# A fused attention and two-layer kernel: all steps put in a new order, found in a replay whose TensorE stops every 127 products

## The chip, the cores and the metric

The kernel runs on one core of a Trainium2 chip. The metric is device microseconds (us) of one execution; lower is better. TensorE (PE) multiplies matrices and loads its stationary operand as a separate step (PEld); VectorE (DVE), ScalarE (ACT) and GpSimd (POOL) do the element-wise work; SyncE (SP) issues the DMAs.

## What is computed

Windowed attention, then a layer with a softmax-weighted activation and a layer norm, then a layer with a sigmoid-gated activation, all in float32:

```
# attention: 4 batches, 8 heads, 576 positions, 64 wide
scores = scale * q @ k.T, masked: heads 0-3 the last 32 positions,
                          heads 4-7 every 4th of the last 128
x = softmax(scores) @ v                      # 2304 tokens x 512

# layer 1: 512 -> 1024 -> 512
h = x @ w_in
solu = h * softmax(h)
ln = (solu - mean) / sqrt(var + 1e-6) * g_ln
x = ln @ w_out

# layer 2: 512 -> 2048 -> 512
h = x @ w_in2
g = h * (1 / (1 + exp(-1.702 * h)))
out = g @ w_out2
```

## The kernel before

**Numbers.** A float32 product is made of three products in a shorter format: high by high, high by low, low by high. So each operand is split: a copy to the short format is its high part, and the difference is its low part. The splits are `split_hi` and `split_lo` for layer 1's weights (L506 to L530), `moe_xh` and `moe_xl` for x, `moe_lnh` and `moe_lnl` for ln (L625, L628), `unit_hi` and `unit_lo` (L696, L700) for the weights of layer 2, and `o_hi` and `o_lo` (L809, L812) for g. The lows of `w_out` carry the factor g_ln and are the tile `wo_l` (L530), the highs `wo_h` (L518 on POOL, L520 on ACT).

**Attention** goes by blocks of one batch and a pair of heads. `att_s` (L276) makes the scores s: up to 64 small products on corners of the array, with the mask added by one product of an identity (L288, L300). The mask, the maximum (`mx`, L324, L327), the exponential and the norm (L362 to L369) follow; `att_t` (L371) transposes the probabilities into a bank called ptp; `att_p` copies them to SBUF (L388, the tiles `diag` and `pt`); and `att_x` (L391) multiplies them by v (xt, L406, L421, L424).

**Layer 1** goes by tiles of 128 tokens. `moe_h` (L549) makes h in two halves of 12 products into one of two large PSUM banks, which is free again when `moe_solu` (L574) has written e (L577). Behind it come the layer norm, four transposes `lt` (L618) and, for each group of tiles, y in 24 products (L638).

**Layer 2** runs in three passes, each over a pair of blocks of 384 tokens, for 8 quads of weight blocks, with seven products in place of eight for each 2 by 2 block. `h_prod` (L762) makes hx and hz; sums and gates follow on DVE, POOL and ACT (L767 to L805), and `o_prod` (L844) multiplies the split g (the tiles `gs`) by the weights `wo` and `w`. The weights of layer 2 are summed and split once (L682 to L700), written to DRAM (`unit_store`, L704, into `wdq` and `wdo`) and read from there for every use (`quad_load` L709; `o_load` L819, the tiles `wo`; `o_load2` L829).

**What sets the order.** Each step is a `Work` of the class `Plan`, with an engine, sometimes other engines that could do it, a cost in us, the steps it needs, and the buffers that it takes and gives back. The list `ORDER` names all 2394 steps in turn; `PICKS` says which steps use a second or third engine. `replay` walks the engines' queues in that order with the costs, and the program is written out in the order of the replayed starts. So both tables, and through the replay also the costs, set what stands before what on each engine. The replay sets one more thing: before a PE step that is marked warm (scores, transposes, xt, h) it counts how long PE would wait, and `stir` (L270) puts that many dummy products of an identity, up to 12, into the bank which the step is about to fill. In the replay PE also waits where a block of instructions must be fetched: every BLOCK products, the first after BLOCK0, no earlier than FETCH us behind the start of the product 32 places ahead.

Of the kernel before, what the change touches and what calls it, by code (L numbers as in the profile page):

```python
# [48 lines left out]
HOP, DMA_RATE, DMA_IN, DMA_OUT, ISSUE, LANES, FETCH, BLOCK, BLOCK0 = 0.035, 360e3, 2.3, 1.0, 0.43, 8, 2.55, 128, 94  # L49
COLD, EARLY, LATE_RATE = 7.5, 60.0, 320e3  # L50
# [14 lines left out]
class Plan:  # L65
# [15 lines left out]
    def replay(self):  # L81
# [15 lines left out]
        port, land, lanes, ld, mms, left = 0.0, 0.0, [0.0] * LANES, 0, [], len(order)  # L97
        while left:
# [32 lines left out]
            if e == "PE":  # L131
# [7 lines left out]
                end, cost = t, w.cost * (2 if t < COLD else 1)  # L139
                for _ in range(w.mm):  # L140
                    if (len(mms) - BLOCK0) % BLOCK == 0 and len(mms) >= 32:
                        end = max(end, mms[-32] + FETCH)
                    mms.append(end)
                    end += cost / w.mm
# [34 lines left out]
def attention_moe_kernel(ctx, tc, qk, qk_last, v, v_last, masks, w_in, w_out, g_ln, w2_in, w2_out, out):  # L179
# [806 lines left out]
    for c in range(8):  # L986
        r, w = at["w", c], done["w", c]
        if (w_out if c >= 4 else w_in).dtype == I64:
# [3 lines left out]
                          ("POOL", 1.115 if c < 4 else 1.35, lambda c=c: split_hi(c, nc.gpsimd))])  # L992
# [11 lines left out]
    for i in range(NTILE):  # L1004
# [24 lines left out]
        w = add(r, "ACT", 1.4, lambda i=i: moe_var(i), [w, z])  # L1029
        w = add(r, "POOL", 0.62, lambda i=i: moe_rs(i), [w])  # L1030
        w = add(r, "ACT", 1.4, lambda i=i: moe_ln(i), [w], port=True,
# [37 lines left out]
    for k in (1, 2, 3):  # L1069
        w_after = [end[n] for n in range(4)] if k < 3 else [closed]  # L1070
        raw, hl = (("raw", k), ("hl", k)) if k < 3 else ("raw", "hl")
        for n, u in enumerate(PARK[k]):
# [8 lines left out]
            for i in range(3):  # L1081
                w = add(r, "POOL", 0.41 if i else 0.69, lambda u=u, i=i: unit_sum(u, i, nc.gpsimd), [w], port=True,
                        also=[("DVE", 0.29 if i else 0.42, lambda u=u, i=i: unit_sum(u, i, nc.vector))])
            lo_ = None
            for part in range(2):
                fin = part == 1

                def split(copy, k=k, u=u, part=part):
# [4 lines left out]
                        also=[("DVE", 0.42 if fin else 0.35, lambda s=split: s(nc.vector.tensor_copy)),  # L1093
# [251 lines left out]
def plan_sequence():  # L1345
# [74 lines left out]
ORDER = [4, 1, 78, 79, 80, 81, 19, 88, 89, 90, 5, 8, 57, 58, 59, 60, 3, 263, 68, 91, 92, 93, 94, 262, 82, 61, 62, 0, 47, 48,  # L1420
# [239 lines left out]
```

## Time and profile before

| | us |
|---|---|
| three runs, median (lowest to highest) | 645.27 (644.74 to 646.63) |
| the profiled execution's own time | 646.25 |
| its span in the trace, first to last instruction | 644.5 |
| PE busy (5065 products) | 626.5 |
| DVE busy | 459.9 |
| ACT busy | 324.2 |
| POOL busy | 257.1 |

The span is that of one execution, recorded by the hardware. An engine's busy time counts its computing instructions alone. The chain of waits goes back from the last instruction to what released it, and so on to the start; its shares say what the time was spent on. A row of a wait tells the engine and line that waited, what came last, the total, how many times, and the longest. In a stretch the columns are its length, the busy time of the engine (with its instructions), the clock that TensorE was granted as a share of full speed (2.4 GHz; one half is 1.2), the share of DMA time and the traffic in GB/s. A few per cent of the products can be missing from the records.

### The profile page before, as it was taken

To read this page: it belongs to the slowest core of one execution; us is meant where nothing else is said; L and a number is where in the kernel's file an instruction comes from. 1 tells how busy PE (TensorE), PEld (TensorE's weight loads), DVE (VectorE), ACT (ScalarE), POOL (GpSimd) and SP (SyncE) were. 2 spreads that over 40 slices of the span, in tenths; PEclk is the share of its full clock that TensorE was granted. 3 is DMA by queue.
4 is the path that set the end of the run, shared out by engine and by line. 5 is a ranking of instruction groups with operands and counts; after the bars stand their busy time and mean duration, and the time that the engine had idled before them with its cause. 6 is when DMAs were issued, how large, how long until landed. Compare 5 with 4: busy or idle time off the path is not lost.

```text
span 644.5 us, 13119 instructions
## 1 busy us (share of the span) xinstructions
PE 626.5 (97%) x5065; PEld 588.8 (91%) x5065; DVE 459.9 (71%) x817; ACT 324.2 (50%) x706; POOL 257.1 (40%) x282
## 2 busy tenths in 40 slices
PE   6889999999999999999999999999999999999997
PEld 3678789889899899999999899999999999999997
DVE  3878998876787976663779969434678963448795
ACT  4689977776475564714547443322454213243331
POOL 2557546454444434655353244204123240026220
PEclk9889999999999999999999999999999999999999
DMA  8899326763667448635988998677898966868584
GB/s 319 319 376 406 116 101 221 255 212 131 216 241 255 178 149 271 235 124 174 321 291 298 343 344 296 236 253 261 275 331 261 330 206 216 290 255 296 186 262 163
DMA packets 65006, 161.36 MB, mean 250 GB/s; under 512 B 6960, under 2 KB 28592, under 8 KB 64944
## 3 DMA queue, kind: packets, MB, share of 16 engines
q1 hardware_dynamic: 64944, 160.53, 71.4%
q8 instruction: 40, 0.66, 0.4%
q14 instruction: 22, 0.18, 0.1%
HBM read 126.42 MB, written 34.08 MB: 249 GB/s over the span
## 4 chain that ended last, share of the span: by engine, by line
PE 82%; DVE 7%; DMA 4%; ACT 3%; issue 2%; POOL 1%; SPq 0%; POOLq 0%; DVEq 0%; ACTq 0%
PE y L638 15%; PE hz L762 15%; PE oz L844 14%; PE hx L762 11%; PE h L557 11%; PE ox L844 9%; PE lt L618 2%; DMA wo<-wdo 2%; DMA wdq<-hl_('q', 7, 1)_0_4305 1%; PE s L292 1%; PE xt L406 1%; DVE e L577 1%; PE ptp L377 1%; DVE gs L812 1%; DMA qk<-in_qk_dram 1%
## 5 line engine op out<-in xcount | busy, mean ns | idle before, releaser
L809 ACT CAST gs<-g 128x384 fp32r<-128x384 f32 x115 | 57.9, 513 | 87.7 <-DVE g L805 37.0
L638 PE MATMUL y<-ln_t,wo_h 128*128 128x384 f32 x384 | 98.4, 337 | 0.0
L762 PE MATMUL hz<-yc,ws 128*128 128x384 f32 x492 | 97.6, 335 | 0.0
L812 DVE TENSOR_TENSOR gs<-g,gs 128x384 fp32r<-128x384 f32 x133 | 80.2, 621 | 21.8 <-ACT gs L809 15.9
L762 PEld LDWEIGHTS hz<-yc,ws 128*128 128x128 f32 x492 | 86.3, 188 | 0.1
L762 PE MATMUL hx<-yc,ws 128*128 128x384 f32 x369 | 74.4, 335 | 0.0
L638 PEld LDWEIGHTS y<-ln_t,wo_h 128*128 128x128 f32 x384 | 69.0, 188 | 0.7
L812 POOL TENSOR_TENSOR gs<-g,gs 128x384 fp32r<-128x384 f32 x35 | 38.8, 1113 | 72.1 <-ACT gs L809 70.4
L762 PEld LDWEIGHTS hx<-yc,ws 128*128 128x128 f32 x369 | 64.8, 188 | 0.2 <-ACT p L767 0.2
L638 PE MATMUL y<-ln_t,wo_l 128*128 128x384 f32 x192 | 64.3, 335 | 0.0
L805 POOL TENSOR_TENSOR g<-g,g 128x384 f32<-128x384 f32 x25 | 28.4, 1142 | 80.2 <-DVE g L805 44.9
L557 PE MATMUL h<-wi_h,xh 128*128 128x512 f32 x144 | 59.0, 410 | 0.9 <-DVE e L577 0.9
L844 PE MATMUL ox<-gs,wo 128*128 128x384 f32 x288 | 55.7, 337 | 1.5 <-DVE gs L812 1.2
L557 PE MATMUL h<-wi_l,xh 128*128 128x512 f32 x144 | 56.6, 393 | 0.0
L557 PE MATMUL h<-wi_h,xl 128*128 128x512 f32 x144 | 56.6, 393 | 0.0
L844 PE MATMUL oz<-gs,wo 128*128 128x384 f32 x288 | 55.2, 335 | 0.1
L844 PE MATMUL oz<-gs,w 128*128 128x384 f32 x288 | 53.4, 336 | 0.0
L844 PEld LDWEIGHTS ox<-gs,wo 128*128 128x128 f32 x288 | 50.2, 188 | 3.0 <-DVE gs L812 2.5
L844 PEld LDWEIGHTS oz<-gs,wo 128*128 128x128 f32 x288 | 50.3, 188 | 0.7 <-DVE gs L812 0.7
L844 PEld LDWEIGHTS oz<-gs,w 128*128 128x128 f32 x288 | 50.1, 188 | 0.7 <-DVE gs L812 0.6
L805 DVE TENSOR_TENSOR g<-g,g 128x384 f32<-128x384 f32 x71 | 43.5, 622 | 5.9 <-ACT g L795 3.4
L795 ACT ACTIVATE g<-g 128x384 f32<-128x384 f32 x72 | 35.0, 520 | 22.6 <-DVE g L771 14.3
(420 smaller groups left out, 1203.2 us busy)
## 6 DMA issues: line engine op xcount, KB each, us to landing
wo<-wdo SPq DMA_DIRECT2D x48, 512.0 KB, 5.5
ws<-wdq SPq DMA_DIRECT2D x41, 512.0 KB, 5.4
w<-wdo SPq DMA_DIRECT2D x72, 256.0 KB, 5.1
ws<-wdq SPq DMA_DIRECT2D x41, 384.0 KB, 4.8
qk<-in_qk_dram SPq DMA_DIRECT2D x14, 528.0 KB, 7.3
v<-in_v_dram SPq DMA_DIRECT2D x14, 512.0 KB, 7.5
out_dram<-ob SPq DMA_DIRECT2D x11, 384.0 KB, 4.7
w_t<-in_w_in_dram SPq DMA_DIRECT2D x8, 512.0 KB, 7.6
```

What stands on the lines that cost most here:

```text
L292: nc.tensor.matmul(ps[QB * j:QB * j + QB, h, m * KW:m * KW + KW], q_[rows, c:c + QB], k_[rows, c:c + KW], start=not masked, stop=not maske ...
L377: nc.tensor.transpose(ps[:, j * P:j * P + P], t[:, 2 * j:2 * j + 2, :].rearrange("p m k -> p (m k)"), ident)
L406: nc.tensor.matmul(o, vW[4 * b + u][:, h, 4 * c + j, :], x, start=True, stop=True, tile_position=(0, 64 * h))
L557: nc.tensor.matmul(hps[i][:, half, :], x[:, kt, :], w[:, kt, fs], start=(kt == 0 and j == 0), stop=(kt == KT - 1 and j == 2))
L618: nc.tensor.transpose(ps[:, j, :], es[i][:, f * P:f * P + P], ident)
L638: nc.tensor.matmul(yps[g, dm][:, 0:TG].rearrange("p (t n) -> p t n", t=GT), w[:, f, ds_], x[:, :, f, :], start=(f == 0 and j == 0), stop=( ...
L762: nc.tensor.matmul(ps[:, 0:TB2], quad_weights(p, q, m, kk, a), yc2[m][:, x, kk, :], start=(m < 4 and kk == 0 and i == 0), stop=(kk == 1 an ...
L795: nc.scalar.activation(g_tile(q, 0, 0) if (half, b) == (0, 0) else src, src, AF.Gelu_apprx_sigmoid)
L805: eng.tensor_tensor(o_block(jj, *o), o_block(jj, *x), o_block(jj, *y_), op)
L809: copy(gsp[jj, m][:, 0], o_block(jj, half, b))
L812: eng.tensor_tensor(gsp[jj, m][:, 1], o_block(jj, half, b), f32(gsp[jj, m][:, 0]), ALU.subtract)
L844: nc.tensor.matmul(ps, w, gsp[jj, m][:, x], start=m < 4 and first and i == 0, stop=last and i == 2, skip_group_check=True)
```

## The change

Constants of the replay and some costs of the planner change, and both tables are new, found in a search that replays with them. No step computes anything else than before. The diff without the rows of the two tables (one line of each stands for it):

```
-HOP, DMA_RATE, DMA_IN, DMA_OUT, ISSUE, LANES, FETCH, BLOCK, BLOCK0 = 0.035, 360e3, 2.3, 1.0, 0.43, 8, 2.55, 128, 94
-COLD, EARLY, LATE_RATE = 7.5, 60.0, 320e3
+HOP, DMA_RATE, DMA_IN, DMA_OUT, ISSUE, LANES, FETCH, BLOCK, BLOCK0 = 0.035, 360e3, 2.3, 1.0, 0.43, 8, 3.2, 127, 95
+COLD, EARLY, LATE_RATE, TURN = 7.5, 60.0, 320e3, 0.095
...
-        port, land, lanes, ld, mms, left = 0.0, 0.0, [0.0] * LANES, 0, [], len(order)
+        port, land, lanes, ld, mms, left, last = 0.0, 0.0, [0.0] * LANES, 0, [], len(order), 0
...
+                kind = 2 if w.mm >= 32 else int(w.mm in (2, 4))
+                if last and not kind or kind == 2 and not last and len(mms) > 12:
+                    end += TURN
+                last = kind
...
-                          ("POOL", 1.115 if c < 4 else 1.35, lambda c=c: split_hi(c, nc.gpsimd))])
+                          ("POOL", 1.115 if c < 4 else 3.25, lambda c=c: split_hi(c, nc.gpsimd))])
...
-        w = add(r, "ACT", 1.4, lambda i=i: moe_var(i), [w, z])
-        w = add(r, "POOL", 0.62, lambda i=i: moe_rs(i), [w])
-        w = add(r, "ACT", 1.4, lambda i=i: moe_ln(i), [w], port=True,
+        w = add(r, "ACT", 1.56, lambda i=i: moe_var(i), [w, z])
+        w = add(r, "POOL", 0.55, lambda i=i: moe_rs(i), [w])
+        w = add(r, "ACT", 1.57, lambda i=i: moe_ln(i), [w], port=True,
...
-                w = add(r, "POOL", 0.41 if i else 0.69, lambda u=u, i=i: unit_sum(u, i, nc.gpsimd), [w], port=True,
+                w = add(r, "POOL", 0.43 if i else 0.86, lambda u=u, i=i: unit_sum(u, i, nc.gpsimd), [w], port=True,
...
-                        also=[("DVE", 0.42 if fin else 0.35, lambda s=split: s(nc.vector.tensor_copy)),
+                        also=[("DVE", 0.42 if fin else 0.545, lambda s=split: s(nc.vector.tensor_copy)),
...
-ORDER = [4, 1, 78, 79, 80, 81, 19, 88, 89, 90, 5, 8, 57, 58, 59, 60, 3, 263, 68, 91, 92, 93, 94, 262, 82, 61, 62, 0, 47, 48,
+ORDER = [4, 1, 78, 13, 79, 80, 14, 81, 82, 19, 88, 89, 90, 8, 57, 58, 59, 0, 47, 91, 92, 93, 5, 68, 60, 61, 62, 3, 262, 263,
...
-PICKS = {53: 1, 65: 1, 67: 1, 74: 1, 75: 1, 96: 1, 105: 1, 124: 1, 137: 1, 156: 1, 158: 1, 169: 1, 181: 1, 191: 1, 200: 1,
+PICKS = {51: 1, 74: 1, 82: 1, 85: 1, 87: 1, 92: 1, 94: 1, 96: 1, 105: 1, 106: 1, 114: 1, 124: 1, 129: 1, 137: 1, 140: 1,
```

Behind its two constants the changed file has four lines more, so its lines carry numbers higher by 4 (L557 is L561). What the new tables do in numbers:

| in the program | before | changed |
|---|---|---|
| products on PE, dummies among them | 5065, 15 | 5070, 20 |
| changes between small and wide products on PE, in the replay's sense | 133 | 127 |
| rows on DVE, ACT, POOL | 793, 570, 277 | 797, 542, 296 |
| pieces of `wo_h` on POOL, ACT | 2, 6 | 0, 8 |
| norm steps of attention (L369, L373 changed) on POOL, DVE | 15, 5 | 9, 11 |
| lows of g (L812) on POOL, DVE | 35, 133 | 41, 127 |

**PE near the 730th product.** The rows of scores (s) with 32 products count twice, so that one group is 64. The 730th product is in the last row of scores of the first list, and falls behind the last transposes (ptp) in the second. Before:

```order
L377 MATMUL ptp_732<-ident,t_612 128x128 x2
L288 LDWEIGHTS ident_b
L288 MATMUL s_736<-mk,ident_b 128x256
L288 LDWEIGHTS ident_b
L288 MATMUL s_736<-mk,ident_b 128x256
L292 MATMUL s_736<-qk_607 32x64 x32
L421 MATMUL xt_0_786<-pt_772,vl_399 64x4x8
```

Changed:

```order
L296 MATMUL s_692<-qk_493 32x64 x32
L381 MATMUL ptp_733<-ident,t_607 128x128 x2
L278 LDWEIGHTS ident_b
L278 MATMUL xt_0_746<-ident_b 128x512
L278 LDWEIGHTS ident_b
L278 MATMUL xt_0_746<-ident_b 128x512
L425 MATMUL xt_0_746<-pt_742,vl_414 64x4x8
L428 MATMUL xt_1_747<-pt_742,vl_414 64x32
```

The score group now stands ahead of the transposes, and the xt behind them has two dummies (L278) in its bank first. At the 349th product it is alike: behind eight transposes came a score, and now come two dummies and an xt.

**DVE between the third and the fourth e of layer 1.** Before:

```order
L577 SCALAR_TENSOR_TENSOR e_1247,mu_1265<-h_1089,e_1247 128x1024
L546 TENSOR_TENSOR xl_1269<-xr,xh_1226 128x512
L530 SCALAR_TENSOR_TENSOR wo_l<-w_t,g_sb,wo_h 128x512 x2
L696 CAST park_hl<-y_early 128x4x128
L530 SCALAR_TENSOR_TENSOR wo_l<-w_t,g_sb,wo_h 128x512 x2
L565 TENSOR_REDUCE nm_1297<-h_1208 128x1
L324 TENSOR_REDUCE mx_1327<-t_1062 128x8
L315 SCALAR_TENSOR_TENSOR t_1337<-s_1310,mk 128x256
L324 TENSOR_REDUCE mx_1357<-t_1337 128x4
L625 CAST ln_t<-lt_0_1301 128x512
L577 SCALAR_TENSOR_TENSOR e_1354,mu_1374<-h_1208,e_1354 128x1024
```

Changed:

```order
L581 SCALAR_TENSOR_TENSOR e_1267,mu_1275<-h_1074,e_1267 128x1024
L534 SCALAR_TENSOR_TENSOR wo_l<-w_t,g_sb,wo_h 128x512 x2
L569 TENSOR_REDUCE nm_1298<-h_1207 128x1
L328 TENSOR_REDUCE mx_1310<-t_1202 128x8
L366 TENSOR_REDUCE sum_eps_110<-t_1067 128x8
L367 TENSOR_REDUCE sx_1338<-sum_eps_110 128x8
L368 RECIPROCAL sx_1338<-sx_1338 128x8
L480 SCALAR_TENSOR_TENSOR y_early<-y_early 128x512
L373 TENSOR_TENSOR t_1067<-t_1067,sx_1338 128x512
L581 SCALAR_TENSOR_TENSOR e_1365,mu_1378<-h_1207,e_1365 128x1024
```

One of two pairs of `wo_l`, a step of x (xl), a copy for layer 2 and a copy of lt have gone from between the two, and a norm of attention and half a weight conversion have come.

**SP ahead of the first o products.** The weight loads (`wo`, two halves for each quad) and the stores of the last split weights (`wdq`, `wdo`). Before:

```order
L673 DMA raw_('o', 5, 1)_4354<-in_w_out_dram 128x1024
L819 DMA wo_0_1_4365<-wdo_124 128x1024
L819 DMA wo_1_1_4367<-wdo_125 128x1024
L819 DMA wo_1_0_4378<-wdo_125 128x1024
L704 DMA wdq_123<-hl_('q', 7, 1)_0_4305 128x768
L819 DMA wo_6_1_4458<-wdo_130 128x1024
L819 DMA wo_6_0_4464<-wdo_130 128x1024
L819 DMA wo_2_1_4489<-wdo_126 128x1024
L819 DMA wo_2_0_4493<-wdo_126 128x1024
L704 DMA wdo_129<-hl_('o', 5, 1)_0_4536 128x768
```

Changed:

```order
L677 DMA raw_('o', 5, 1)_4315<-in_w_out_dram 128x1024
L708 DMA wdq_123<-hl_('q', 7, 1)_0_4280 128x768
L708 DMA wdq_123<-hl_('q', 7, 1)_1_4286 128x1024
L823 DMA wo_0_1_4339<-wdo_124 128x1024
L823 DMA wo_0_0_4381<-wdo_124 128x1024
L823 DMA wo_1_1_4384<-wdo_125 128x1024
L823 DMA wo_1_0_4395<-wdo_125 128x1024
L823 DMA wo_6_1_4454<-wdo_130 128x1024
L823 DMA wo_6_0_4459<-wdo_130 128x1024
L708 DMA wdo_127<-hl_('o', 3, 0)_0_4489 128x768
L823 DMA wo_2_1_4511<-wdo_126 128x1024
L823 DMA wo_2_0_4514<-wdo_126 128x1024
```

The store of quad 7's last weights goes ahead of the `wo` loads, and one store of (o,3,0) ahead of the load of `wo_2`.

## Rows read from the trace of the kernel before

**Rows 1.** Page, part 1: busy us (share of the span), instructions.
```profile
span 644.5 us, 13119 instructions
PE 626.5 (97%) x5065; PEld 588.8 (91%) x5065; DVE 459.9 (71%) x817; ACT 324.2 (50%) x706; POOL 257.1 (40%) x282
```

**Rows 2.** Page, part 4: the chain that ended last, by engine.
```profile
PE 82%; DVE 7%; DMA 4%; ACT 3%; issue 2%; POOL 1%; SPq 0%; POOLq 0%; DVEq 0%; ACTq 0%
```

**Rows 3.** Stretches: length, PE busy (products), clock, DMA share, GB/s.
```profile
0.00:13.92 13.92, 7.87 (x222) 1.00 0.88 305
13.92:19.99 6.07, 3.83 (x127) 1.00 1.02 405
19.99:36.65 16.66, 13.51 (x381) 0.90 0.86 295
36.65:39.74 3.09, 3.08 (x100) 0.56 1.00 407
39.74:160.00 120.26, 119.03 (x1523) 1.00 0.60 220
160.00:340.00 180.00, 179.96 (x1007) 1.00 0.65 224
340.00:380.00 40.00, 38.37 (x212) 1.00 0.92 329
380.00:640.90 260.90, 260.87 (x1501) 1.00 0.77 261
```

**Rows 4.** Waits of PE: us in total, times, longest us.
```profile
PE s L292 <- issue: 3.7, 2, 1.8
...
PE s L288 <- DVE mx L327: 2.1, 1, 2.1
...
PE h L557 <- DVE e L577: 0.9, 1, 0.9
PE xt L406 <- DVE diag L388: 0.9, 1, 0.9
```

**Rows 5.** Page, part 3: the queue that fetches instructions.
```profile
q8 instruction: 40, 0.66, 0.4%
```

**Rows 6.** Timeline of PE, 19 to 41 us: start, length, line, what.
```profile
21.63 1.93 PE L406 MATMUL xt<-diag,v 128*64 128x64 f32 x32
26.08 1.15 PE L406 MATMUL xt<-diag,y_early 128*64 128x64 f32 x32 [0.18 <-ACT diag L388]
```

**Rows 7.** Chain, 100 to 180 us: start, length, what.
```profile
119.80 2.95 PE h L557 x12
129.02 2.77 PE h L557 x12
```

**Rows 8.** Groups of instructions: count, busy us, mean ns, idle before.
```profile
L274 PE MATMUL s<-ident_b 128*128 128x512 bf16 x10 | 4.3, 596 | 2.6 <-POOL ident_b L201 2.6
L518 POOL TENSOR_SCALAR wo_h<-w_t,g_sb 128x512 fp32r<-128x512 f32 x2 | 3.7, 1877 | 0.0
```

**Rows 9.** Timeline of DVE, 68 to 82 us.
```profile
70.15 1.22 DVE L577 SCALAR_TENSOR_TENSOR e<-h,e 128x1024 f32<-128x1024 f32 x1
73.56 2.46 DVE L530 SCALAR_TENSOR_TENSOR wo_l<-w_t,g_sb,wo_h 128x512 fp32r<-128x512 f32 x2
79.05 1.22 DVE L577 SCALAR_TENSOR_TENSOR e<-h,e 128x1024 f32<-128x1024 f32 x1
```

**Rows 10.** Chain, 325 to 385 us.
```profile
339.18 8.25 DMA wdq<-hl_('q', 7, 1)_0_4305
347.45 4.24 DMA wo<-wdo
360.51 2.59 DVE gs L812 x2
```

**Rows 11.** Timeline of DVE, 350 to 366 us.
```profile
351.87 1.03 DVE L812 TENSOR_TENSOR gs<-g,gs 128x384 fp32r<-128x384 f32 x2
360.43 2.66 DVE L812 TENSOR_TENSOR gs<-g,gs 128x384 fp32r<-128x384 f32 x2
```

**Rows 12.** Timeline of POOL, 355 to 366 us.
```profile
361.47 1.20 POOL L812 TENSOR_TENSOR gs<-g,gs 128x384 fp32r<-128x384 f32 x1
```

280 rows, old and new, of tables (ORDER, PICKS) are left out of this document.

## The prediction

> **What bounds the kernel now.** I read the page's first part, then the chain that ended last, then the stretches of the span, and the waits of TensorE (PE) last. PE is busy for 626.5 of the span's 644.5 us [rows 1], and 82% of the chain of waits is PE's own work [rows 2]. The number of real products does not change (5065 before, 5070 after, and the five more are dummy products of `stir`), so the change can only win what PE does not use: 644.5 − 626.5 = 18.0 us, less what lies before its first product and after its last. The stretches say where that is [rows 3]. From 160 to 340 us PE is busy for 179.96 of 180.00, and from 380 to 640.9 us for 260.87 of 260.90: no order wins anything there. What is left lies in four places: 0 to 39.74 us (39.74 − 7.87 − 3.83 − 13.51 − 3.08 = 11.45 idle, part of it the wait for the first data), 39.74 to 160 us (1.23 idle), 340 to 380 us (1.63 idle) and the end behind the last product (644.5 − 640.9 = 3.6, the same three steps in both orders).
>
> **The first 40 us stop by count.** The page counts 40 instruction fetches [rows 5]. The cuts of [rows 3] stand where PE resumes after its three long stops, and the products between the cuts are 222 = 95 + 127, then 127, then 381 = 3 × 127. So a stop falls behind the 222nd, the 349th and the 730th product, which is what the planner's new constants, 95 and 127, say; with 94 and 128 its replay was off by a product more with each block. The waits name two of them as issue, 3.7 us in two, and one as a wait for `mx`, 2.1 us [rows 4]; but this one too begins right at a cut, behind the 349th product, so I take it for a fetch as well. The other multiples, 476 and 603 among them, show no stop: a fetch hides where PE has slow products to do. The granted clock in the 3.09 us behind the third stop is 0.56, half speed of 2.4 GHz being 1.2 [rows 3]; 32 small products took 1.93 us in such a stretch behind the second stop and 1.15 at full clock [rows 6]: 0.8 us more.
>
> **The change part by part.**
>
> *Changes of kind on PE (TURN).* The planner now charges 0.095 us where PE goes from small products to wide ones or back. The order has 127 such changes where it had 133. Twelve products of h took 2.95 us behind scores and 2.77 us behind transposes [rows 7], so a change from small to wide cost 0.18. Of the six fewer, one is of that sort. For the others no row gives a price; I bound them by 0 and by the same 0.18, and take 0.05. Sum: 0.18 + 5 × 0.05 = −0.4, between 0 and −1.1. Nothing hides this, since PE is what waits last.
>
> *The first 40 us.* All three stops stay where the count puts them; the first (46th product of the fourth score) has the same rows ahead of it in both orders. What changes is what stands behind them. At 349 the score gives way to two dummy products and a group of xt; at 730 it gives way to two dummies and the small xt pairs. An xt must wait for the copy of its probabilities: the longest such wait is 0.9 us [rows 4], and inside a stop it is free. Against this stand five more dummy products. The planner sets them only into a wait that it foresees; where that wait is there, they cost nothing, and where it is not, five of them at 0.43 (4.3 us for ten, the dummies' own group, [rows 8]) are 2.2 us. I take a third of the 0.9: −0.3. Ends: −3.0 (the 0.9, and the stop of 2.1 hidden as well) and +2.9 (a fourth stop of 2.1, and 0.8 at half clock).
>
> By the Trainium skill, "Runtime: NRT & Kernel Launch", section Instruction fetch mechanics, the sequencer fetches the next 16 KiB block while the present one runs and crossing a boundary is "mostly hidden"; by this alone the place of the boundaries would be worth nothing, this term 0, and no fourth stop could come. The trace bears out the block (0.66 MB in 40 fetches, [rows 5]) and "mostly" (37 of 40), but not that the rest is free: three cost about 2 us each.
>
> *The phase of h and layer 1, 40 to 160 us.* One wait stands out: h waits 0.9 us for the fourth e, which must leave before a bank comes free [rows 4]. On VectorE (DVE) the third and fourth e start 8.90 us apart (79.05 − 70.15), and among what lies between is a pair of `wo_l` that took 2.46 us [rows 9]. In the new order one such pair stands between these two e, not two, and `wo_l` work goes ahead of the third e; short reductions and one attention step of the same stretch come in. By the rows' kinds I count 5.5 us there. So e is early by some 3 us, and the 0.9 goes whole. What is late next is unknown: six norm steps of attention go from GpSimd (POOL) to DVE, which is busy for 71% of the span [rows 1]. I let half of it come back: −0.6, between −1.2 (all idle time of the stretch) and +0.9 (a new wait as long as the old).
>
> *The longer split on GpSimd.* The cost 1.35 → 3.25 for `split_hi` is right by the trace: two pieces of `wo_h` took 3.7 us, 1.88 each [rows 8]. The search now gives both to ACT, which is busy for half of the span [rows 1]. No PE row of [rows 4] waits for `wo_h`, so the 3.7 us leave POOL hidden: 0, and if the cover went, at most the 1.88 of one. The other new costs only steer the search.
>
> *Start of the o products, 340 to 380 us.* 1501 products in 260.87 us are 0.174 each [rows 3]; 40 us would hold 230, and 212 ran, so at most 18 × 0.174 = 3.1 us are lost, and at least the 1.63 idle. In the chain a store of (q,7,1)'s first part takes 8.25 us to land among weight loads, and DVE is the next link with two lows of g at 2.59 us [rows 10]. On SP the store now goes ahead of all `wo` loads instead of behind three of them; what it is moved past are loads that are wanted later than it, and the load of `wo_2` goes behind one more store. On POOL stand six more lows of g (35 to 41), which spare DVE 0.5 each. But the two lows of g took 1.03 us elsewhere [rows 11] and 2.66 us while POOL ran one of its own [rows 11, 12]: a collision costs 2.66 − 1.03 = 1.6. I take half of the 3.1: −1.5. Ends: −3.1, and +1.6 for one more collision on the path with nothing won.
>
> By the Trainium skill, "SBUF — State Buffer", DVE and GpSimd hold a shared port pair by an exclusive lock for a whole instruction. It speaks against more lows on POOL. By it the price would be POOL's own 1.20 and the upper end +1.2; the trace shows a little more, 1.6.
>
> *Everything else* (POOL 19 rows more, ACT 28 fewer, from 160 us on): hidden by a PE that is never idle there: 0. If the cover went, the price is that of a low on POOL in place of DVE, some 0.6 (1.20 against half of 1.03, [rows 11, 12]) each.
>
> **Sum:** −0.4 − 0.3 − 0.6 − 1.5 = −2.8 us. The profiled execution took 646.25 us (1.75 over its span, which I leave as it is): 643.45. It stands 0.98 over the median of 645.27, so against the median the forecast is **642.5 us**.
>
> **The rivals.** 0.3% of 645.27 is 1.94 us, about what a measurement of this kernel can tell from no change; so faster is below 643.3 and slower above 647.2.
>
> *Forecast*, 0.52: 642.5.
>
> *Nothing of note*, 0.33: the three stops cost what they cost, since the order keeps them, and at the start of o the earlier store is paid back by two collisions at 1.6 on DVE. Left are 0.4 of the changes of kind and 0.3 of the third e: 645.27 − 0.7 = 644.6. For it: PE's loss is small everywhere, and two thirds of the stretches offer none. Against it: the chain runs through exactly that store. The skill's page on the fetch would give this case too, with its first term at 0.
>
> *A fourth stop*, 0.15, slower: behind the 476th product. The 32 products ahead of it were five dummies, four transposes and 23 small ones; now they are three dummies, four transposes and 25 small ones, so up to 2 × 0.43 = 0.9 us of the work that hid this fetch is gone. If the fetch is not over, PE stops for up to 2.1 us and falls to half clock for another 0.8. If the other places give only the 0.4 of the kinds: 645.27 + 2.9 − 0.4 = 647.8. It puts the kernel on the slower side as long as all other gains together stay under 2.9 − 1.94 = 1.0. For it: nothing in the row of before says how much time that fetch had to spare. Against it: neither the 476th nor the 603rd showed a stop, and xt products wait for copies anyhow, which gives a fetch time.
>
> **How the numbers follow.** The forecast's own range is 639.5 to 645.0 (all of the start of o won and part of a stop hidden: 1.6 + 1.4 below; nothing won at the start of o, and a wait of 1.0 elsewhere: 1.5 + 1.0 above). For 8 in 10 I take 639.5 to 647.0, which holds the second case and the lower part of the third. Faster 0.52, same 0.33, slower 0.15.
>
> **What would show it.** Right: stops at the cuts 222, 349 and 730 by count; no wait of h for e near 80 us; no `wo_h` on POOL; from 340 to 380 us PE idle under 0.6 us and no chain link over 5 us from that store; 160 to 340 us and 380 us to the last product busy as before. Wrong: a stop of about 2 us at the 476th or 603rd product, or a stop lost; lows of g on DVE of 2.6 us a pair between 345 and 375 us; a wait of h or y for DVE over 1 us between 45 and 160 us; or new idle time from 160 us on, which I exclude.

## The result: slower by 1.0%, and the profile after

The changed kernel took 653.22 us (median of 6 runs, 651.55 to 654.18), the kernel before 646.71 beside it (6 runs, 644.74 to 647.69): ratio 1.0101, 95% interval 1.0078 to 1.0123. That is 6.5 us slower, where 2.8 us faster was forecast. The profiled execution took 653.58 us with a span of 651.8. Its page, busy time and chain:

```profile
span 651.8 us, 13135 instructions
PE 629.2 (97%) x5070; PEld 589.8 (90%) x5070; DVE 471.9 (72%) x821; ACT 311.1 (48%) x680; POOL 271.9 (42%) x301
...
PE 78%; DVE 6%; DMA 3%; ACT 2%; issue 1%; SPq 0%; DVEq 0%; ACTq 0%
```

PE is busy for 2.7 us more than in [rows 1] (some 1.6 of it the dummies, the rest half clock), and idle for the rest of the 7.3 us that lie between the two spans. The stretches of PE, cut again where it goes on behind a stop and at the same stages (length, busy time with products, granted clock, DMA share, GB/s):

```profile
0.00:13.05 13.05, 7.71 (x223) 0.99 0.87 302
13.05:21.59 8.54, 5.62 (x126) 0.62 1.02 397
21.59:27.76 6.17, 4.72 (x127) 1.00 1.03 402
27.76:38.31 10.55, 8.13 (x254) 1.00 0.74 253
38.31:160.00 121.69, 119.62 (x1605) 0.99 0.64 221
160.00:345.00 185.00, 184.61 (x1030) 1.00 0.64 221
345.00:395.00 50.00, 45.60 (x252) 1.00 0.88 302
395.00:648.20 253.20, 253.19 (x1458) 1.00 0.77 258
```

Against [rows 3] there are now four stops instead of three: the products between the cuts are 223, 126, 127 and 254 = 2 × 127, so the 476th has one too (one product's shift at the first two is as the records have it). The second stretch ran at a granted clock of 0.62; before, the lowest of the first three was 0.90. From 345 to 395 us PE is idle for 4.40 us; from 340 to 380 it was 1.63. Only the last stretch has no more than before.

PE's waits (total, times, longest), against [rows 4]:

```profile
PE xt L278 <- issue: 3.6, 2, 2.2
...
PE oz L848 <- DMA wo<-wdo: 2.1, 1, 2.1
PE s L296 <- issue: 1.9, 1, 1.9
PE ptp L381 <- DVE t L373: 1.5, 1, 1.5
PE xt L410 <- issue: 1.4, 1, 1.4
PE ox L848 <- DVE gs L816: 1.3, 2, 0.9
PE oz L848 <- DVE gs L816: 0.8, 1, 0.8
PE h L561 <- DVE e L581: 0.7, 1, 0.7
PE xt L410 <- ACT diag L392: 0.6, 1, 0.6
```

The three rows of issue hold the four stops, 6.9 us of them instead of 5.8 (issue and `mx` of [rows 4]). New or longer are a wait of the transposes for a norm step on VectorE (1.5), of xt for ScalarE's copy (0.6), and of the o products for `wo` (2.1) and for lows of g (2.1 in three waits, 1.2 in two before). The wait of xt for VectorE's copy fell from 0.9 to 0.3. A wait of h for an e is still there, 0.7 for 0.9, but for another e (told with the prediction's term for h).

**Where the time went.** To compare two programs whose products stand in different orders, I lay PE's products end to end, each at its usual length and dummies left out (some 610 us of work, the same in both), and read at what time a given amount of work was reached. The table gives by how much the later kernel is late against the profile of before, and where it became so; "again" is the second profile of the new order, below.

```
work done, us     at (before)   new order   again   new until layer 2   old until layer 2
0 to 60           82 us           +3.3       +3.0         +3.4                +0.2
60 to 280         303 us          +0.2       +0.9         +3.7 (seam)         +1.7 (seam)
280 to 380        407 us          +4.0       +4.1         +0.2                +3.3
380 to the end    641 us          -0.2       -0.4         -0.1                -0.4
```

So there are two losses, one before 82 us and one between 303 and 407 us. The last two columns are experiments that splice the two orders. Read at more places, the first profile of the new order loses 2.2 us up to 40 us, 1.1 from there to 82, 0.2 to 303, 1.0 to 344 and 3.0 to 407, and wins 0.2 behind it; the second has 0.9, 2.0, 0.9, 2.1, 1.9 and again a gain, of 0.4. So the two sums agree better than the places: how a loss is shared between neighbouring stretches changes from one execution of the program to the next.

### The profile page after: what moved, and what is told of

Its sections match the earlier page's. It is cut to its first block, busy times and chain, and to the rows that moved or that the text cites. A ratio compares the mean times of both kernels' runs of the same rounds, so it can differ in the third digit from the quotient of the medians.

```text
span 651.8 us, 13135 instructions
## 1 busy us (share of the span) xinstructions
PE 629.2 (97%) x5070; PEld 589.8 (90%) x5070; DVE 471.9 (72%) x821; ACT 311.1 (48%) x680; POOL 271.9 (42%) x301
## 4 chain that ended last, share of the span: by engine, by line
PE 78%; DVE 6%; DMA 3%; ACT 2%; issue 1%; SPq 0%; DVEq 0%; ACTq 0%
PE y L642 15%; PE hz L766 14%; PE oz L848 14%; PE hx L766 11%; PE h L561 10%; PE ox L848 9%; PE lt L622 2%; DMA ws<-wdq 2%; DVE gs L816 1%; DMA wo<-wdo 1%; DVE g L809 1%; PE xt L410 1%; ACT t L356 1%; DVE ln_t L632 1%; DVE e L581 1%
## 5 line engine op out<-in xcount | busy, mean ns | idle before, releaser
L813 ACT CAST gs<-g 128x384 fp32r<-128x384 f32 x105 | 53.1, 513 | 84.7 <-DVE g L809 30.9
L816 POOL TENSOR_TENSOR gs<-g,gs 128x384 fp32r<-128x384 f32 x41 | 44.7, 1096 | 108.4 <-DVE gs L813 57.8
L816 DVE TENSOR_TENSOR gs<-g,gs 128x384 fp32r<-128x384 f32 x127 | 78.0, 634 | 16.1 <-ACT gs L813 11.7
L561 PE MATMUL h<-wi_h,xh 128*128 128x512 f32 x144 | 59.1, 410 | 1.0 <-DVE e L581 0.7
L561 PE MATMUL h<-wi_h,xl 128*128 128x512 f32 x144 | 57.0, 396 | 0.0
L561 PE MATMUL h<-wi_l,xh 128*128 128x512 f32 x144 | 56.8, 395 | 0.0
```

Of the source, the lines that this page charges most:

```text
L561: nc.tensor.matmul(hps[i][:, half, :], x[:, kt, :], w[:, kt, fs], start=(kt == 0 and j == 0), stop=(kt == KT - 1 and j == 2))
L813: copy(gsp[jj, m][:, 0], o_block(jj, half, b))
L816: eng.tensor_tensor(gsp[jj, m][:, 1], o_block(jj, half, b), f32(gsp[jj, m][:, 0]), ALU.subtract)
```

## The experiments

All kernels are built on the kernel before, with tables of their own. The dummies are written down for each step, so that no replay changes their number:

```
-            self.stirs = w.stirs
+            self.stirs = STIRS.get(w.key[1], 0)
```

### Where the losses lie: four splices

In each, the steps up to a point have the order and engines of one table, and the rest those of the other; where a buffer was not free yet, a step was passed by the next that could go.

```
-ORDER = [4, 1, 78, 79, 80, 81, 19, 88, 89, 90, 5, 8, 57, 58, 59, 60, 3, 263, 68, 91, 92, 93, 94, 262, 82, 61, 62, 0, 47, 48,
+ORDER = [4, 1, 78, 13, 79, 80, 14, 81, 82, 19, 88, 89, 90, 8, 57, 58, 59, 0, 47, 91, 92, 93, 5, 68, 60, 61, 62, 3,
...
```

New up to the first h (117 steps):

> The new order up to the first h, then the old one. Theory (the loss is made in four places and stays): PE is late by what the start loses, +2.2 us against the kernel before, with four stops instead of three in the first 40 us. Rival (lateness of the start is made up, since later steps have slack, and all the loss is at the start of the o products): 0, within 0.5 us.

Measured 650.30 us, ratio 1.0069 (1.0045 to 1.0092): +4.3 us, twice what was expected. In its profile PE is already 3.7 us late at 42 us, where the new order itself was 2.6 and 0.7 us late in its two profiles.

New up to about 80 us (287 steps):

> The new order up to about 80 us, then the old one. Theory: +2.2 of the start and +1.1 of waits of h and xt between 45 and 75 us, so +3.3 us. Rival (made up later): 0, within 0.5 us.

Measured 652.02 us, 1.0098 (1.0076 to 1.0119): +6.1 us; of it 1.8 us are a new wait at the seam (`lt` for e on GpSimd, at 90 us).

New up to layer 2 (959 steps), and old up to layer 2:

> The new order up to the first product of layer 2, then the old one. Theory: +3.5 us, the start of the o products as in the kernel before (about 1.6 us idle from 340 to 380 us, moved by 3.5). Rival (all of it at the start of o, whatever stands ahead): under 0.5 us. A third: lateness of the weight stores is already made before layer 2, then the loss at the start of o comes back here too: +6 to +7 us.

> The old order up to the first product of layer 2, then the new one. Theory: the start and the middle as before, +0.7 us from hx waiting for ws near 311 us and +3.0 us at the start of the o products, +3.7 us in all. Rival (lateness at the start of o comes from layer 1's end and from the start): 0 to +1 us.

Measured 655.23 us, 1.0153 (1.0126 to 1.0181), and 652.19 us, 1.0101 (1.0074 to 1.0128). The totals are above what was expected, in part because a seam has a cost of its own (the rows marked so in the table). But the lateness in the table, behind the seam, is clear: with the old order from layer 2 on, the loss between 303 and 407 us is gone (+0.2), whatever the start was; with the new one it is there (+3.3) behind an old start. PE's waits from 290 to 400 us, first new until layer 2, then old until layer 2:

```profile
PE hz L762 <- ACT y L642: 1.4, 1, 1.4
PE ox L844 <- DVE gs L812: 1.2, 2, 0.6
PE hz L762 <- POOL yc L749: 1.0, 1, 1.0
```

```profile
PE ox L844 <- DVE gs L812: 1.4, 2, 0.9
PE hx L762 <- DMA ws<-wdq: 1.2, 2, 0.8
PE oz L844 <- DVE gs L812: 1.0, 2, 0.8
```

The two hz rows of the first are its seam; the rest is as before. The losses stay where they are made and are not made up later: the rival of the first two expectations falls, and so does the third reading of the third one, that the stores are already late before layer 2. The last expectation holds in its sum, not in its parts: 1.8 us are lost before 344 us and 1.5 behind it, where 0.7 and 3.0 were expected.

### What a stop waits for: fewer loads in flight

In the trace's records of the DMA queues one can see each of the 40 instruction fetches start. PE goes on 2.2 to 2.6 us behind that start, in every stop of every run that a fetch ends. But the start itself comes 1.3 to 6.1 us after PE crossed the boundary before, in the two profiles. Times in us, for the boundaries of the first 45 us; "reached" is the start of the last product before the boundary:

```
                    before                               new order
boundary   reached  fetch starts  goes on     reached  fetch starts  goes on
222         11.89      11.71       13.93       10.94      10.68       13.06
349         17.66      17.53       20.00       19.96      19.18       21.60
476         25.50      22.93       25.52       26.10      25.43       27.77
603         30.16      26.80       30.21       31.65      29.33       31.93
730         34.59      34.35       36.66       35.83      35.99       38.32
```

Theory: a fetch waits behind the data that are in flight. To test it, SyncE waits in the old order before a load until the one D places ahead has landed:

```
+                    if i.engine == mybir.EngineType.SP and "DMA" in type(i).__name__.upper():
+                        if 8 <= len(sent) < 42:
+                            tc.add_manual_dep(i, sent[len(sent) - 2], mybir.DependencyInfo(
+                                mybir.DependencyClass.Sync, mybir.DependencyReason.DATA), reason="few in flight")
+                        sent.append(i.name)
```

> The old order; from the 9th to the 42nd load SP waits until the load two places ahead has landed, so that at most about 1 MB is in flight in the first 45 us, instead of 1.4 to 3 MB. Theory (an instruction fetch of PE waits behind the data in flight: 3.6, 2.9 and 4.1 us after the crossing of the boundary before, and PE goes on 2.3 us after its start): the fetch starts at most 2.6 us after the crossing, the three stops of 2.0, 2.3 and 2.1 us shrink to 1.0, 1.2 and 0.5 us, and the kernel is 2 to 4 us faster. Rival 1 (the fetch waits for something else): the stops stay at 2 us, time within 1 us or slower. Rival 2 (fewer in flight let the DMA engines go idle): the stops shrink, but data come late and the kernel is 1 to 5 us slower.

> As the run before it, with three loads in flight (about 1.5 MB). Theory: the fetch starts 2.5 to 3.9 us after the crossing; stops shorter by 0 to 1 us each, 0 to 2 us faster, no idle DMA. Rival 1: stops as before, 0. Rival 2: half the loss of the run with two.

Measured 671.22 us, 1.0382 (1.0354 to 1.0410), and 654.10 us, 1.0110 (1.0081 to 1.0138). The theory held for the stops at the first two boundaries: with three in flight the fetches start 1.2, 3.1, 1.0, 2.8 and 2.9 us behind the crossing instead of 3.8, 3.6, 2.9, 1.3 and 4.1 (with two 0.5, 2.1, 0.2, 1.9 and 0.4), and PE's idle time at the five boundaries is 0.02 us or less. The third stop went for another reason as well: late data brought PE to the 730th product at 39.4 us instead of 34.6, when the fetch, which started at 35.26 instead of 34.35, was over. No wait for issue is left in the view of PE's waits up to 45 us, whose two longest rows with three in flight are

```profile
PE s L297 <- DMA qk<-in_qk_dram: 4.8, 3, 1.7
PE ptp L382 <- POOL t L374: 2.8, 2, 2.3
```

Rival 2 held for the time: data come late instead. The stretches of the run with three in flight, then of the kernel before (the last columns are clock, DMA share and GB/s):

```profile
0.00:15.00 15.00, 8.54 (x244) 1.00 0.81 278
15.00:30.00 15.00, 11.56 (x347) 0.89 0.87 280
30.00:45.00 15.00, 11.09 (x254) 0.89 0.89 294
```

```profile
0.00:15.00 15.00, 8.77 (x243) 1.00 0.89 313
15.00:30.00 15.00, 11.87 (x356) 0.89 0.88 322
30.00:45.00 15.00, 12.91 (x347) 0.89 0.98 365
```

365 GB/s have become 294 from 30 to 45 us. The start is bound by the loads nearly as much as by the fetches, and taking the stops away only shows the waits that lay behind them. Two attempts to have the one without the other, with three in flight for the 9th to the 17th load only, and with five throughout (`len(sent) < 17`; `len(sent) - 5`):

> The old order; only from the 9th to the 17th load SyncE waits until the load three places ahead has landed. With three in flight for all of the first 45 us the 350th product came 1.0 us earlier (19.0 for 20.0 us) and only the later data came late. Theory (fetch behind the data in flight): the stops at the 222nd and 349th product stay short (under 0.5 us), the third comes back, 0 to 1 us faster than the kernel before. Rival (each load that waits is made up for nowhere): 1 to 2 us slower.

> The old order with at most five loads in flight (2.6 MB) from the 9th to the 42nd. Theory: in flight at the crossings were 2.8, 2.4, 1.4, 0.7, 2.4 and 3.1 MB, so this binds at the first and behind the third stop alone: stops within 0.5 us of before, time within 1 us. Rival (data come late): 1 to 3 us slower.

Measured 648.93 us, 1.0044 (1.0028 to 1.0060), and 647.18 us, 1.0016 (0.9995 to 1.0036). The first is 2.2 us slower, as its rival had it: no stop is left at the 222nd and the 349th product, but PE reached the latter at 19.88 us instead of 17.66, and stops of 1.9, 0.6 and 1.5 us came at the 603rd, 730th and 857th. The second had its 20 us of work done 1.4 us earlier in its profile, which is inside the scatter told below, and is no faster. No version beat the kernel before.

Over the first six boundaries of 20 traces, the fetch starts on average 1.3 us behind the crossing with under 0.8 MB in flight (about a fifth of the 120 fetches), 2.7 us with 0.8 to 1.5 MB, and 4.0 us with more (about two thirds). The scatter in the last group is large, up to 6.1, and most of the traces share one of two starts, so the amount is not all there is to it.

### What makes the new start late

Two theories: N, the norm step that went from GpSimd to VectorE makes transposes wait, and PE falls to half clock; F, the fetches decide. Undone are first the two norm steps alone, then loads in flight (four), dummies, and all 16 steps of the first 37 us that had changed their engine:

```
-PICKS = {51: 1, 74: 1, 82: 1, 85: 1, 87: 1, 92: 1, 94: 1, 96: 1, 105: 1, 106: 1, 114: 1, 124: 1, 129: 1, 137: 1, 140:
+PICKS = {51: 1, 74: 1, 85: 1, 87: 1, 94: 1, 96: 1, 105: 1, 106: 1, 114: 1, 124: 1, 129: 1, 137: 1, 140:
...
-STIRS = {78: 9, 95: 1, 86: 2, 52: 1, 66: 2, 73: 3, 148: 2}
+STIRS = {78: 9}
```

> The new order with the first two of the norm steps that went from GpSimd to VectorE back on GpSimd. Theory N (the wait of 1.5 us of the first transposes for the norm on VectorE, right behind the first stop, makes TensorE idle for 3.4 of 5.2 us, its clock falls to half until 20 us, and that makes the 349th product late): the wait falls under 0.4 us, the clock stays full from 10 to 20 us, TensorE goes on behind the 349th product at 20.0 to 20.5 us instead of 21.6 to 22.2, and the time falls by 1 to 2 us against the new order (651 to 652). Theory F (that stop ends when the fetch comes, which starts at 19.2 to 19.7 us behind 2.5 MB in flight, whatever TensorE did before): it still goes on at 21.6 to 22.2 us, with a longer stop, and the time stays within 0.7 us.

> The new order with at most four loads in flight (2.1 MB) from the 9th to the 42nd. Theory F: the fetch for the 349th product starts 1 us or more earlier (18 us or before), TensorE goes on behind it at 20 to 21 us, and the stops in the first 40 us, 8 us in the new order, fall to 4 us or less; the time falls by 0 to 2 us, less what late data cost. Theory N: the wait for the norm and the half clock are as before, and so is the time of the 349th product, 21.6 us or more.

> The new order without the 11 dummy products behind the first nine. Theory F: every boundary moves up to 11 real products on, the stops at the fetches stay as many (the fetch decides), time within 0.7 us of the new order. Rival (the dummies themselves stand in the way at half clock, 0.6 us each two): 1 to 2 us faster.

> The new order; the 16 steps of the first 37 us (of the replay) that had changed their engine are back on the old one, the two norm steps among them. Theory N (engines make the start late): the loss of 2 to 4 us in the first 45 us goes at least by half, 650 to 651.5. Theory F (loads and fetches do): within 1 us of the new order, 652 to 654.

Measured: norm steps back 654.51 us, 1.0105 (1.0073 to 1.0137); four in flight 656.08, 1.0151 (1.0101 to 1.0201); no dummies 655.17, 1.0139 (1.0114 to 1.0163); all engines back 660.17, 1.0208 (1.0177 to 1.0240). None is faster than the new order. With the norm steps back, PE's waits up to 45 us and its stretches:

```profile
PE s L292 <- issue: 2.2, 1, 2.2
PE xt L274 <- ACT pt L385: 2.1, 1, 2.1
PE ptp L377 <- POOL t L369: 0.8, 1, 0.8
PE xt L274 <- issue: 0.8, 1, 0.8
```

```profile
15.00:20.00 5.00, 4.70 (x106) 0.50 1.03 412
20.00:25.00 5.00, 4.21 (x49) 0.54 1.03 403
```

The wait is only half gone (0.8), the clock is at half speed all the same, and PE goes on behind the 349th product at 21.76 us, in the range that F gave (21.6 to 22.2): the fetch for it started at 19.25 us. So the run did not set up what N asks for, but a second profile of the new order (the last run below) speaks against N: there the granted clock was 1.00 up to 16 us, 0.56 and 0.59 to 20, and 1.00 again to 46 us, and still PE went on at 21.38 us and was 3.0 us late at 82 us. With four in flight F is not borne out either: that fetch started at 18.87 us instead of 19.18, where F wanted 18 or earlier, and PE went on at 22.58, where F wanted 20 to 21; only the waits for issue fell to 4.0 us, as F had it. Without dummies the stops stay (2.0, 1.5, 1.4, 0.05 and 1.2 us from reached to going on), as F has it, and the ratio of 1.0139 can't be told from the 1.0101 and 1.0130 of the new order's two measurements. All engines back made the transposes wait 4.4 us for a norm on GpSimd: new order and new engines belong together. So the fetch is what ends last at the 349th product, but no run took the loss of the new start away.

Why that one fetch waits 5 to 6 us with the new start and 3.6 to 3.8 with the old one, and how far a start is settled by its program, was asked of two last runs. In the first, only SyncE's loads of the first 45 us have the old order:

```
-ORDER = [4, 1, 78, 13, 79, 80, 14, 81, 82, 19, 88, 89, 90, 8, 57, 58, 59, 0, 47, 91, 92, 93, 5, 68, 60, 61, 62, 3,
...
```

> The new order on all engines but SyncE, whose loads of the first 45 us stand in the old order (but that the load of the second block end stays behind two others). Theory F (what is in flight at a crossing decides how long a fetch waits): the fetch for the 349th product starts 3.6 to 4 us behind the crossing as in the old order, not 5 to 6, and TensorE goes on there at 20 to 20.5 us, not at 21.6 to 22.2; data come in another order than the new order of scores wants, so waits for qk or v of 1 us and more may come, and the time is 651 to 654. Rival (the order of the loads is of no account): the fetch starts 5 to 6 us behind the crossing as before.

> The new order once more, program for program. If the start is settled by the program, the work that was done at 42.6 us in the profile of the new order is done within 0.5 us of that again, and the time is 652 to 654 us. If it is not, the start moves by 1 to 3 us between executions, as it did in the ten runs that share its first 36 us (41.6 to 45.5 us).

Old loads: 668.22 us, 1.0342 (1.0316 to 1.0367). The fetch for the 349th product started 3.6 us behind the crossing, as F said, and the stop at the 222nd was 0.02 us. But the data came in a sequence that the new order cannot use:

```profile
PE ptp L377 <- DVE t L369: 9.8, 1, 9.8
PE s L292 <- DMA qk<-in_qk_dram: 5.4, 2, 4.5
```

That is 14 us worse, far outside the 651 to 654 expected. PE crossed the 222nd product only at 16.42 us instead of 13.06, and the fetch, at 19.98 us, started no earlier than the 19.18 of the new order. So the run does not show that the order of the loads decides; why that fetch waits 5 to 6 us stays open.

The new order again: 654.94 us, 1.0130 (1.0100 to 1.0160). It had 20 us of work done at 41.16 us, the first profile at 42.64. So the same program's start moves by 1.5 us from one execution to another. Of the two answers on record the second holds. Three profiles with the old start had that work done at 38.03, 40.40 and 40.73 us, eight with the new start at 41.16 to 45.48 (mean 43.2). At 82 us the two profiles of the new order differ by only 0.3 us, but six that share its program up to layer 2 are 3.0 to 6.0 us late there.

### What makes the start of the o products late

```
-    1, 1103: 1, 1104: 1, 1107: 1, 1109: 1, 1281: 1, 1282: 2, 1283: 1, 1284: 1, 1285: 2, 1287: 1, 1288: 1, 1289: 1,
...
```

The 50 steps that had changed their engine there are put back on the old ones, or the old order is taken with the new engines:

> The new order; the 50 steps around the start of the o products (330 to 392 us of the replay) that had changed their engine are back on the old one, in the new order. Theory A (the six collisions of DVE with POOL and the work moved to DVE make the last splits late): the loss of 3.0 us between 345 and 395 us goes, 3 us faster than the new order, +3.5 us against the kernel before. Theory B (the order of the splits does it): the loss stays, +6 to +7 us against the kernel before.

> The new order up to about 327 us of the replay, the old one from there, but the 50 steps on the new engines. Theory B (the order of the splits does it): the loss of 3.0 us at the start of the o products goes, +3.5 to +4.5 us against the kernel before. Theory A (engines): it stays, +6 to +7 us.

Measured 658.46 us, 1.0176 (1.0157 to 1.0196), and 658.17 us, 1.0171 (1.0150 to 1.0193). Both theories fail: between 303 and 407 us the first lost 7.7 us, the second 6.0, the new order itself 4.0. Of these, 2.8, 1.9 and 1.0 us were lost before 344 us, where the edits have hardly begun, so 4.9, 4.1 and 3.0 (1.9 in the second profile of the new order) belong to the stage itself. The second also has a seam there, whose own cost it can't separate. Neither half of the change could be shown to be the culprit; each was worse without the other. Then the lows of the last three weight units were left out, in both orders:

```
+        if u in (("o", 3, 0), ("o", 3, 1), ("o", 5, 1)):
+            nc.scalar.copy(l_, x)
+        else:
+            eng.tensor_tensor(l_, x, f32(h_), ALU.subtract)
```

> The new order; the lows of the last three weight units of layer 2 ((o,3,0), (o,3,1), (o,5,1); five on VectorE and one on GpSimd at the start of the o products) are left out, and ScalarE writes a copy of the sum in their place. Theory C (at the start of o VectorE has more than it can do, and these splits stand among the lows of g, so the last store and with it the last load of wo come late): VectorE is relieved of 3 us, the store of (o,3,1) comes 2 to 3 us earlier, and of the 3.0 us lost between 345 and 395 us at least 2 are back: 2 to 3 us faster than the new order, about +4 us against the kernel before. Theory D (the loads and stores on SyncE or the waits for ScalarE's highs set it): within 1 us of the new order, +6 to +7 us.

> The same lows left out in the old order, where all six are on VectorE. Theory C: VectorE is relieved of 3.6 us, the 1.6 us that TensorE is idle there go: 0.5 to 1.6 us faster than the kernel before. Theory D: within 0.5 us.

Measured 654.91 us, 1.0138 (1.0116 to 1.0160), and 647.08 us, 1.0008 (0.9994 to 1.0022). PE's waits from 290 to 400 us, without the lows, and in the second profile of the new order:

```profile
PE hx L765 <- DMA ws<-wdq: 1.7, 2, 1.3
PE oz L847 <- DVE gs L815: 1.7, 2, 0.9
PE ox L847 <- DVE gs L815: 0.9, 1, 0.9
```

```profile
PE hx L762 <- DMA ws<-wdq: 1.5, 2, 0.9
PE ox L844 <- DVE gs L812: 1.4, 2, 0.9
PE oz L844 <- DVE gs L812: 0.8, 1, 0.8
PE ox L844 <- DMA wo<-wdo: 0.5, 1, 0.5
```

The wait for `wo` is gone, but it was only 0.5 in the second profile of the new order too, where hx waited 1.5 for `ws`; the stretch loses 3.4 us as against 4.0 and 4.1, and the old order gains nothing. Eight profiles have the new sequence unchanged from layer 2 on, and they lose 2.3 to 4.5 us between 303 and 407 us; eight with the old one there stand between −0.4 and +0.3. So 3.4 is in the middle of what the new order does anyhow, and theory C is not borne out. What is shown is that the loss comes from the new sequence behind the start of layer 2; which of its steps makes hx wait for `ws` and the o products for g stays open.

## Why the prediction was wrong, step by step

- **Changes of kind, −0.4:** not seen. From 60 to 280 us of work, where most of them lie and PE is saturated, the new order is 0.2 and 0.9 us later, not earlier. The term is smaller than what else moves there.
- **The first 40 us, −0.3 (ends −3.0 and +2.9):** wrong, +2.2 (0.9 in the second profile), and the rival of the fourth stop happened, at the 476th product: PE reached it 0.7 us behind the start of the fetch, and stood for 1.67 us. In the old order the fetch had 2.6 us. The reason that the rival gave (less work ahead of the boundary) is half of it: PE took 4.50 us from the 349th product to the 476th instead of 5.50, and the fetch started 3.8 us behind the crossing instead of 2.9. What failed is the step "All three stops stay where the count puts them". I took the stops for fixed lengths at places that a count gives, so that only what stands behind them could change. The long ones end 2.2 to 2.5 us behind the start of a fetch, and that start is not fixed: it comes 1.3 to 6.1 us behind the crossing of the boundary before. At the 349th product it was 6.1 us instead of 3.6, though about as much was in flight at the two crossings (2.2 and 2.4 MB), and why stays open. So PE, which left the 222nd 0.9 us earlier than before, left this one 1.6 us later (21.60 for 20.00). Its own waits (1.5 us for a norm step, then half clock) made it reach the place at 19.96 us for 17.66, but by then the fetch set the time. The step on xt held: its wait for VectorE's copy went from 0.9 to 0.3.
- **By the Trainium skill**, "Runtime: NRT & Kernel Launch", section Instruction fetch mechanics, the crossing of a block is "mostly hidden", by which alone this term would have been 0. The traces agree from 54 us on: there a fetch starts 60 to 163 products ahead of its boundary in both kernels, and no stop is left. Before that they differ, with 5.8 and 6.9 us of stops, and the measurement decides.
- **h and layer 1, −0.6 (ends −1.2 and +0.9):** wrong sign; of the 3.3 us that are lost up to 82 us, 1.1 are lost behind 40 us (2.0 in the second profile). The sum has a slip too: half of 0.9 is 0.45; 0.6 is half of the stretch's idle time. For the fourth e the step held: it starts 7.82 us behind the third instead of 8.90, and its h (at 83.67 us) does not wait. But the wait came back one e earlier, 0.72 us of h at 75.93 us for the third. What failed is that work put ahead of the third e was priced at nothing: six `wo_l` stand between the second and the third e instead of four, and the maximum of h (nm) that the third needs starts behind the last of them, 2.2 us behind its h instead of 1.0. ScalarE's exponential follows 1.5 us behind that maximum (1.2 before), and e right behind it. And xt waited 0.65 us for a copy on ScalarE (the last of PE's waits above). VectorE from the last `wo_l` to the third e, and its fourth e; then the exponential for the third:

```profile
67.93 2.73 DVE L534 SCALAR_TENSOR_TENSOR wo_l<-w_t,g_sb,wo_h 128x512 fp32r<-128x512 f32 x4
70.58 1.21 DVE L569 TENSOR_REDUCE nm<-h 128x1 f32<-128x1024 f32 x1
74.55 1.22 DVE L581 SCALAR_TENSOR_TENSOR e<-h,e 128x1024 f32<-128x1024 f32 x1
82.37 1.22 DVE L581 SCALAR_TENSOR_TENSOR e<-h,e 128x1024 f32<-128x1024 f32 x1 [0.56 <-ACT e L575]
```

```profile
73.31 1.12 ACT L575 ACTIVATE e<-h,nm 128x1024 f32<-128x1024 f32 x1
```

- **The longer split, 0:** as said. All eight `wo_h` are on ScalarE, 0.77 us each, and nothing waits for them:

```profile
L524 ACT ACTIVATE wo_h<-w_t,g_sb 128x512 fp32r<-128x512 f32 x8 | 5.7, 768 | 0.0
```

- **The start of the o products, −1.5 (ends −3.1 and +1.6):** wrong by sign and beyond its end, +3.0 against −1.5 (+1.9 in the second profile). The store of (q,7,1) did go ahead, and no chain link of 8.25 us from it is left ([rows 10]). What I did not follow is what stood behind it: the stores of (o,5,1) went from 353.40 and 354.47 us to 358.46 and 364.46, that of (o,3,1)'s second part from 364.96 to 370.91, and the last load of `wo` came 6.5 us later, with PE only 4 us late:

```profile
305.81 5.85 DMA ws<-wdq
314.10 5.21 DMA ws<-wdq
375.76 7.06 DMA wo<-wdo
```

  The ledger asked only which of the old links would go, not which step would be the next to come last; that loads of `wo` now stand behind one more store was named and priced at nothing. The collisions were more, as feared: on VectorE six operations of 0.7 to 0.8 us too long in 42 us of that stage. Their price of 1.6 was a misreading, though: the 2.66 us of [rows 11] are two lows of 1.37, each beside a step of GpSimd, one of which [rows 12] does not have, so one collision costs 0.8, less than either price set for it (1.6 and 1.2):

```profile
360.12 1.25 POOL L805 TENSOR_TENSOR g<-g,g 128x384 f32<-128x384 f32 x1 [1.57 <-DVE gs L812]
```

  Putting the engines back made the stage worse, so the collisions are not shown to be what it lost by.
- **From 160 us on, 0:** wrong by 1.0 us before the o products (2.1 in the second profile): hx waits for `ws` behind the two loads above, at 311 and 319 us. I excluded new idle time there because the old order had none; a new order of the splits is reason enough for some.
- **The rival on the slower side** had its place right and its price too low (647.8): it was one of several losses. The chance of 0.15 for slower was far too small. A kernel whose PE is busy for 97% under an order found by search has little to win and much to lose when all of the order moves.

## What to carry to other kernels

When a whole schedule is replaced, do not price it by the waits of the old trace that go: price each stage by what will come last next, and let the range reach on the slower side by as much as the old schedule's slack is unknown. Order and engine choices of one search belong together: the three runs that took the order of one table with the engines of the other, in one stage, were slower than either kernel (658.17 to 660.17 us). Where many small products run while loads fill the DMA queues, count instruction fetches as a resource whose latency can grow with the data in flight, as it did in these traces; but a start that is bound by loads as well gains nothing when the fetches alone are relieved.

## What the runs showed of the hardware that was not expected

An instruction fetch of PE started on average 1.3 us behind the crossing of the boundary before with under 0.8 MB in flight, and 4.0 us with over 1.5 MB; PE went on 2.2 to 2.6 us behind the start. With at most three loads in flight no stop of over 0.02 us was left at the first five boundaries, though PE also came later to the last of them. And the same program reached the same work at 41.16 us in one profile and at 42.64 in another: this phase is not settled by the program to better than 1.5 us, between a fifth and a quarter of the loss that was to be explained.
